# A forgetting-attention and gated feed-forward kernel with its opening rearranged: loads, fillers, gate rows and table load

## The chip, the cores and the metric

The kernel runs on one core of a Trainium2 chip. The metric is the device time of one execution in microseconds (us). TensorE (PE) multiplies matrices; VectorE (DVE), ScalarE (ACT) and GpSimd (POOL) work element by element; SyncE (SP), ACT and POOL issue DMA transfers, SP and ACT on one kind of queue and POOL on another. Each engine carries out its own instructions in the order of the program and waits on semaphores for the others.

## The reference, cut to what matters

```python
B, H, S, D = 8, 8, 576, 64                        # batches, heads, positions, head width
scores = q @ k.T / 8                              # per batch and head
cum    = cumsum(log(clip(f, 1e-4, 1)))            # along the positions
scores = where(causal, -1e9, scores + cum[:, None] - cum[None, :])
attn   = softmax(scores) @ v                      # 4608 x 512, heads side by side
g      = attn @ w_gate                            # 512 -> 1536
out    = ((g * sigmoid(g)) * (attn @ w_val)) @ w_out   # 4608 x 512, float32
```

## The kernel before

**Planning.** The kernel doesn't issue its work directly. It lists operations (`op`), each with the engines that may do it, an estimated duration, what it comes after, which buffers it takes, a key, an earliest time (`ready`) and, for a transfer, an estimated duration (`dma`). `Plan.run` then plays these through in time: an engine that is free takes the ready operation with the smallest key, and instructions are written out in that order. A table `ORDER` overrides keys of single operations. So any change of an estimate, a key or an earliest time moves the order on every engine, and the order that comes out is fixed in the program. Where PE has nothing, the plan puts in `dummy` products (L995), the fillers, from `ID_AT` on and not after `IDLE_TO`.

**Heads and pairs.** Batch 0 and batch 1 are loaded with two heads stacked on the two halves of the partitions. For batch 0, four loads `ld_quad` (L541, q and k for each of two groups) go out on POOL; each serves two pairs of heads (jj = 0, 1 for one group, 2, 3 for the other). PE transposes them piece by piece (`turn_two`, L549, 18 products of 64x64 for each pair and operand), and ACT or DVE copies the result from PSUM to the tile QK (`straighten_two`; the copy is L323 on ACT and L325 on DVE).

**Scores.** `score2` forms the scores of a pair (L708), first its first part (bank 0: keys and queries 0 to 255 as far as causal, 256 + 128 columns) and later the second part (banks 1 to 3, 1216 columns in five pieces). The decay terms are added by further products into the same bank. For the second part this is one product per piece (L716) of the key's gate rows `KG` with a tile `QG[jj]` that holds this pair's query gates; `choose` makes `QG[jj]` from the cumulative sum (L387 on ACT, L389 on DVE). For the first part there are two products (L719, L720): `KG` with a column of ones, and a one-hot column of the identity with `QS`, the scaled cumulative sum of all pairs, which one ACT instruction makes (`up`, L382). ACT takes the exponential (L724), POOL masks the diagonal blocks (L733), PE multiplies with V (`weigh`, L747), DVE divides (L754, L759), PE transposes the result (L764), and the copy to xT follows.

**Gates.** `gates` loads the gate input f of batch 0 four times into 64 partitions (`ld_f`, four transfers of 16 rows, two each on SP and ACT), clips it (DVE, L355), takes logarithms (ACT, L358), forms the cumulative sum (DVE, L362) and splits it into bfloat16 parts in `KG` (DVE, L367, L371, L375, L378), in two parts of 256 and 320 columns. f of the other six batches (`flat`, in the tile ot) takes another way: clip, logarithm, a write to memory (`regroup`, L352) and a read back in another layout (L350), then a cumulative sum and five steps (`later`) much later. SP also copies gate rows and rows of ones into QK for batch 1 (`dec_in`, L399; L477). The ones come from a fill of a part of the tile ot (L466, DVE). L517 is a tiny exponential that loads ACT's table for it ahead of use.

**Feed-forward.** For each of nine token tiles of 512: the two products with the weights (L892, four per unit), tanh on ACT (L896), two DVE steps (L900, L903), and the product with w_out (L907). Units of the first tile can run as soon as its tokens and the weights (L888) are there, and are what PE does between attention steps from then on. Later batches' q and k are narrowed in memory by POOL (`narrow`) and transposed by DMA on SP, at times set by `PACE0`, `PACE`, `PACE_A` and `LEAD`.

Of the kernel before, what the change touches and what calls it, by code (L numbers as in the profile page):

```python
# [9 lines left out]
F32 = mybir.dt.float32  # L10
# [24 lines left out]
class Plan:  # L35
# [41 lines left out]
    def run(self, idle=None):  # L77
# [31 lines left out]
        while left:  # L109
# [46 lines left out]
            for e in engines:  # L156
                while busy[e] <= t + 1e-9:
# [27 lines left out]
                    if o.dma is not None:  # L185
# [3 lines left out]
                        push(max(end + (0.2 if o.tag == "f" else 0.9), T_SW if e == "POOL" else 0.0), "queue", o)  # L189
# [27 lines left out]
PACE0 = 58.0  # L217
LEAD = 14.0
# [3 lines left out]
def kernel(ctx, tc, q, k, v, f, w_gate, w_val, w_out, out):  # L222
# [51 lines left out]
    warm = sb("warm", [1, 1], F32)  # L274
    bank = [banks.tile([P, MT], F32, name=f"ps{i}") for i in range(8)]
# [14 lines left out]
    QS = xT[:, 3, 3 * S + D : 3 * S + D + HALF]  # L290
# [90 lines left out]
    def up(e, c):  # L381
        nc.scalar.activation(QS, cum[:, c], AF.Copy, scale=8.0)  # L382

# [31 lines left out]
    def gates(parts, key):  # L415


        lds = [op(("ACT" if n % 2 else "SP", 0.45), ld_f, n, key=-40, dma=0.1, packet=100, tag="f") for n in range(4)]
        ld1 = op(("SP", 0.5), ld_f, None, key=-39, dma=LD1, packet=50, ready=LD1_AT, behind=lds[2:3], tag="f1")
# [6 lines left out]
        for i, c in enumerate(parts):  # L426
# [8 lines left out]
            u = op(("ACT", 0.15 + w / 1100), up, c, after=[s], key=kk, tag="up") if i == 0 and ONEHOT else None  # L435
            done.append([[a, o_one, u] if jj in ONEHOT and not i else
# [3 lines left out]
        outs = [op(("SP", SPi), dec_in, n, j, after=ends, key=-7 + 0.1 * j, dma=0.05, packet=50, tag="decin") for j in range(2) for n in range(4)]  # L440
# [13 lines left out]


    def blank(e, what):
# [8 lines left out]
        elif what == "ones":  # L465
            E[e].memset(ones.bitcast(F32), ONE2)  # L466
# [36 lines left out]
        else:  # L503
            if what != "rest":
                nc.vector.memset(VB[what][:, :, :, D:].bitcast(F32), ONE2)
            if what:
                nc.vector.memset(VB[0 if what == "rest" else what][LAST:, NB - 1], 0.0)
# [4 lines left out]
    o_id = op(("POOL", 0.6), lambda e: make_identity(nc, ident[:, :]), key=-18)  # L512
    o_past = op(("DVE", 0.1), blank, "past", key=-29.2)
# [5 lines left out]
    o_vb = [op(("DVE", 0.4 if i else 0.12), blank, i, key=(-29.5, VB1_KEY)[i] if i < FIRST else 40 + 2000 * i, ready=0 if i == 0 else 10 if i < FIRST else 15) for i in range(NVB)]  # L519
    o_qkz = op(("DVE", 0.3), blank, "qk", key=QKZ_KEY)  # L520
    o_pt = op(PT_ENG, blank, "pt", key=PT_KEY, ready=10)
    o_ones = op(ONES, blank, "ones", key=ONES_KEY, ready=10)
    o_edge = op(("SP", SPi), blank, "edge", after=[o_qkz], key=900, dma=0.2, ready=22)
    o_out1 = [op(("SP", SPi), blank, (w, j), after=[o_ones], key=1, dma=0.05, packet=50, ready=4) for j in range(2) for w in range(2)]
# [108 lines left out]
    def four(g, key):  # L633
# [3 lines left out]
        for j in range(2):  # L637
            jj = 2 * g + j
            q_ready[0, jj] = []
            for x in range(2):  # L640
                kk = key + STEP[j] + x
                bt = Buf("t", ("f", TURN_F))
                o2 = op(("PE", 0.41), turn_two, jj, x, bt, after=[o1[x], o_id], take=[bt], key=kk, tag=("turn", 0, jj, x))
# [52 lines left out]
    def score2(e, b, jj, i, bs):  # L696
# [14 lines left out]
        for n, (kt, q0, w, c) in enumerate(segs):  # L711
            for u in range(2):
                r, end = slice(D * u, D * (u + 1)), n == len(segs) - 1
                o, keys = ps(bs[u])[:, c : c + w], KG_ALL[r, kt * P : (kt + 1) * P]
                if i or jj not in ONEHOT:
                    nc.tensor.matmul(o, keys, QG[jj][r, q0 : q0 + w], start=False, stop=end)  # L716
# [98 lines left out]
    def attention2(b, key, parts):  # L815

        bx = {}
        for n, (bks, qb, nq) in enumerate(parts):
            ahead = len(parts) > 1 and n == 0
            got = {}  # L820
            for jj in range(4):
# [4 lines left out]
                for m, i in enumerate(bks):  # L826
                    bs = [Buf("s", ("f", F_UNTIL)) for _ in range(2)]
                    segs = [x[2] for x in BANKS[i]]
                    cost = mm(*segs) * (3 if not i and jj in ONEHOT else 2) + 0.105
# [163 lines left out]
    def dummy(i):  # L993
        z = bank[bank_of[i[0]] + i[1]]
        nc.tensor.matmul(z[:, :HALF], ident, ident.unsqueeze(1).to_broadcast([P, 2, P]), start=True, stop=True)  # L995
# [9 lines left out]
TWARM = 7.5  # L1005
ID_AT = 2.72
SPARE = 0.12
LD1_AT = 0.0
QUAD0 = (1.85, 1.25, 1.65, 1.4)
# [10 lines left out]
ONEHOT = (0, 1, 2, 3)  # L1020
CLIP1_KEY = -24.9
PT_ENG = ('DVE', 0.66)
PT_KEY = 3
ONES = ('DVE', 0.3)
# [107 lines left out]
```

## Time and profile before

| what | value |
|---|---|
| runs shown | 382.79, 383.37 and 384.94 us (median 383.37) |
| the profiled execution's own time | 382.61 us |
| its span, first to last instruction | 380.9 us |
| PE busy | 372.1 us |
| DVE, ACT, POOL busy | 218.8, 211.2, 141.2 us |
| HBM traffic over the span | 146 GB/s |

The span is 1.7 us shorter than the execution's own time, as starting and ending lie outside it. A row of a timeline has the start, the duration from the first start to the last end of a merged group, engine, line, operation, output and input, shapes, and the count; in brackets stands idle time just before it and what ended it. PE's records include the passage through the array, so rows that follow each other overlap.

### The profile page before, as it was taken

Reading aid. Unit: us, or ns where it says so; the run is one execution under the profiler, and the core shown is the slowest. Engines: PE = TensorE matmul, PEld = TensorE weight load, DVE = VectorE, ACT = ScalarE, POOL = GpSimd, SP = SyncE. Lnnn points to the kernel's source line nnn. Section 1 sums busy time; section 2 is a strip of 40 time slices with the busy share of each in tenths; the row PEclk is TensorE's granted clock in tenths of the full one; section 3 lists DMA queues with packets and bytes.
Section 4 is the critical chain, followed back from the end, with each engine's and each line's share of the span. In section 5 each row is a group of like instructions: output and inputs, shape, how many; then the busy total and the mean of one; then the engine's idle time right before and its main releaser. Section 6 shows DMA issues by size and latency. Waiting matters only on the chain.

```text
span 380.9 us, 8367 instructions
## 1 busy us (share of the span) xinstructions
PE 372.1 (98%) x3127; PEld 206.4 (54%) x3127; DVE 218.8 (57%) x458; ACT 211.2 (55%) x433; POOL 141.2 (37%) x368
## 2 busy tenths in 40 slices
PE   5999999999999999999999999999999999999997
PEld 3668555555555555545554565555654444444444
DVE  7899794467616772387327651576327815743860
ACT  5999745266566574835674577547763323323322
POOL 8896446236443463526452356513430000000000
PEclk9999999999999999999999999999999999999999
DMA  9999997997588989999799979992321011002003
GB/s 129 187 194 201 211 209 150 167 235 143 117 194 162 207 130 161 206 188 183 129 203 203 178 123 187 234 220 55 94 74 45 0 57 55 0 29 83 3 0 111
DMA packets 125319, 51.96 MB, mean 136 GB/s; under 512 B 112110, under 2 KB 119726, under 8 KB 124510
## 3 DMA queue, kind: packets, MB, share of 16 engines
q1 hardware_dynamic: 108782, 36.18, 47.8%
q0 software_dynamic: 16288, 15.14, 26.6%
q8 instruction: 24, 0.39, 0.4%
q14 instruction: 17, 0.14, 0.1%
q10 hardware_dynamic: 208, 0.11, 0.1%
HBM read 38.56 MB, written 17.07 MB: 146 GB/s over the span
## 4 chain that ended last, share of the span: by engine, by line
PE 89%; DMA 5%; ACT 2%; DVE 2%; issue 1%; POOL 1%; DVEq 0%; POOLq 0%
PE ps L892 46%; PE ps L907 25%; PE ps L690 9%; PE ps L747 7%; DMA lnf_d<-ot 4%; DMA QK<-lnf_d 1%; ACT PT L724 1%; PE ps L995 1%; PE ps L708 1%; PE ps L764 0%; DVE th L900 0%; ACT QK L323 0%; POOL xT L541 0%; PE ps L549 0%; DVE QK L362 0%
## 5 line engine op out<-in xcount | busy, mean ns | idle before, releaser
L896 ACT ACTIVATE th<-ps 128x512 f32<-128x512 f32 (+1 forms) x112 | 65.1, 582 | 83.9 <-PE ps L892 82.8
L892 PE MATMUL ps<-xT,wg 128*128 128x512 bf16 (+1 forms) x448 | 111.4, 371 | 0.2 <-DVE th L900 0.2
L892 PE MATMUL ps<-xT,wv 128*128 128x512 bf16 (+1 forms) x448 | 111.4, 371 | 0.1
L900 DVE SCALAR_TENSOR_TENSOR th<-th,ps 128x512 f32<-128x512 f32 (+1 forms) x112 | 74.6, 666 | 60.2 <-ACT th L896 59.8
L907 PE MATMUL ps<-wo,hh 128*128 128x512 bf16 (+3 forms) x468 | 105.8, 362 | 0.0
L724 ACT ACTIVATE PT<-ps 128x512 bf16<-128x512 f32 (+2 forms) x192 | 91.7, 510 | 18.6 <-PE ps L690 12.1
L903 DVE TENSOR_TENSOR hh<-th,ps 128x512 bf16<-128x512 f32 (+1 forms) x112 | 74.7, 668 | 11.8 <-PE ps L892 0.9
L733 POOL TENSOR_SCALAR_AFFINE_SELECT PT<-PT 128x128 bf16<-128x128 bf16 (+1 forms) x192 | 53.2, 282 | 55.5 <-ACT PT L724 50.4
L892 PEld LDWEIGHTS <-wv 128*128 128x128 bf16 x448 | 42.7, 97 | 41.6 <-issue 0.5
L690 PE MATMUL ps<-QK 68*128 68x256 bf16 (+4 forms) x392 | 64.8, 260 | 0.1
L892 PEld LDWEIGHTS <-wg 128*128 128x128 bf16 x448 | 42.3, 97 | 40.5 <-issue 0.5
L907 PEld LDWEIGHTS <-hh 128*128 128x128 bf16 x468 | 41.2, 97 | 34.4
L733 POOL TENSOR_SCALAR_AFFINE_SELECT PTa<-PTa 128x256 bf16<-128x256 bf16 x64 | 26.5, 418 | 85.3 <-ACT PTa L724 84.1
L754 DVE RECIPROCAL rc<-ps 128x5 f32<-128x5 f32 (+2 forms) x68 | 12.9, 190 | 68.3 <-PE ps L747 68.1
L911 ACT ACTIVATE ot<-ps 128x512 f32<-128x512 f32 (+3 forms) x39 | 22.0, 565 | 45.2 <-PE ps L907 43.7
L747 PE MATMUL ps<-VB,PT 128*128 128x65 bf16 x768 | 45.1, 193 | 0.0
L747 PEld LDWEIGHTS <-PT 128*128 128x128 bf16 x768 | 36.8, 97 | 14.4 <-POOL PT L733 1.3
L690 PEld LDWEIGHTS <-QK 68*128 68x128 bf16 x392 | 31.4, 97 | 17.2 <-issue 0.4
L724 ACT ACTIVATE PTa<-ps 128x384 bf16<-128x384 f32 x64 | 30.8, 488 | 14.3 <-PE ps L690 13.2
L759 DVE TENSOR_TENSOR xn<-ps,rc 128x320 bf16<-128x320 f32 (+2 forms) x72 | 32.2, 453 | 2.1
L325 POOL CAST VB<-natv 128x512 bf16<-128x512 f32 (+1 forms) x32 | 19.7, 631 | 0.0
L747 PEld LDWEIGHTS <-PTa 128*128 128x128 bf16 x192 | 13.1, 97 | 11.3 <-issue 1.1
(71 smaller groups left out, 153.2 us busy)
## 6 DMA issues: line engine op xcount, KB each, us to landing
out_dram<-ot SPq DMA_DIRECT2D x35, 256.0 KB
natv<-in_v_dram SPq DMA_DIRECT2D x25, 256.0 KB
qk_d<-in_q_dram POOLq DMA_DIRECT2D x24, 144.0 KB, 3.8
qk_d<-in_k_dram POOLq DMA_DIRECT2D x24, 144.0 KB, 4.4
wg<-in_moe_w_gate_dram POOLq DMA_DIRECT2D x3, 512.0 KB, 12.1
wv<-in_moe_w_val_dram POOLq DMA_DIRECT2D x3, 512.0 KB, 13.5
wo<-in_moe_w_out_dram POOLq DMA_DIRECT2D x4, 384.0 KB, 16.7
xT<-in_q_dram POOLq DMA_DIRECT2D x4, 288.0 KB, 8.8
```

What stands on the lines that cost most here:

```text
L325: E[e].tensor_copy(dst, src)
L690: nc.tensor.matmul(s[:, c : c + w], QK[:KR, hqk[p].i, 1, j * S + kt * P : j * S + (kt + 1) * P], QK[:KR, hqk[p].i, 0, j * S + q0 : j * S + ...
L724: nc.scalar.activation(place(h, i)[:, OFFS[i] : OFFS[i] + c], ps(bs)[:, :c], AF.Exp, scale=0.125)
L733: nc.gpsimd.affine_select(out=d, in_=d, pattern=pat, compare_op=ALU.is_ge, fill=0.0, base=0, channel_multiplier=-1,)
L747: nc.tensor.matmul(o[:, lo : lo + D + 1], pt[:, c : c + P], VB[hvb[b].i][:, kt, hb, : D + 1], start=first and n == 0, stop=last and n == l ...
L759: nc.vector.tensor_mul(XN[bx.i][:, qb : qb + nq, j], o, r)
L892: nc.tensor.matmul(ps(bf)[:, :n], w[:, ko, fc * P : (fc + 1) * P], xT[:, ko, t0 : t0 + n], start=(ko == 0), stop=(ko == KD - 1))
L896: nc.scalar.activation(TH[bt.i][:, :n], ps(bf)[:, :n], AF.Tanh, scale=0.5)
L900: nc.vector.scalar_tensor_tensor(out=t, in0=t, scalar=1.0, in1=ps(bf)[:, :n], op0=ALU.add, op1=ALU.mult)
L903: nc.vector.tensor_mul(HH[bh.i][:, lo : lo + n], TH[bt.i][:, :n], ps(bf)[:, :n])
L907: nc.tensor.matmul(ps(bf)[:m, c], HH[hs[fc].i][:, lo : lo + m], wo[:, fc, c], start=(fc == 0), stop=(fc == KF - 1))
L911: nc.scalar.activation(OT[bo.i][:m, c], ps(bf)[:m, c], AF.Copy, scale=0.5)
```

## The change

- Loads of f for batch 0: two transfers of 32 rows (a source that repeats the 16 rows), one on SP and one on ACT, in place of four of 16.
- The fillers read a new tile `idle`, filled by DVE at the start, in place of the identity; `ID_AT` goes from 2.72 to 0.8.
- `ONEHOT1 = (0, 1)`: pairs 0 and 1 take the two-product form in the second part too. A second `QS` is made by a second `up`, and `choose` is left out for these two pairs in that part.
- Fills can be done by ACT (`fill32`): the ones rows go to ACT in the resulting order; the padding of the second V buffer stays on DVE and comes earlier.
- The round trip of the other batches' logarithms may start earlier (`ready` 6 and 16 in place of 21 and 27).
- Estimates of the plan: PE's `turn_two`, the warm-up time, the time from issue to queue of the f loads, issue times of SP, load times; `PACE0` 57 for 58 and `LEAD` 16 for 14; a new `ORDER` table.

The order that results differs on every engine. At the start it is, by line of the new kernel (which are 8 to 10 higher): POOL issues k and q of the first group, makes the identity, issues q and k of the second, four chunks of V, then batch 1's first loads; before it was q, a chunk of V, k, identity, q, k and the rest of V. ACT does four logarithms, the ones fill, the logarithm for the other batches, the table load, then a copy, `up`, five copies, the second `up`, two exponentials, a copy and exponentials; before, the table load came after two copies. SP issues one ones row, the write L353, three ones rows, five gate rows, the read L351, three gate rows, then V loads. PE has 18 fillers ahead of the first transposes (11 before), 35 in all (22), and the first product of the feed-forward comes after more of the attention.

```diff
-                        if o.tag[0] != "turn":
-                            dur *= self.clock(t)
+                        dur *= self.clock(t)
...
-                        push(max(end + (0.2 if o.tag == "f" else 0.9), T_SW if e == "POOL" else 0.0), "queue", o)
+                        push(max(end + (0.7 if o.tag == "f" else 0.9), T_SW if e == "POOL" else 0.0), "queue", o)
...
-PACE0 = 58.0
-LEAD = 14.0
+PACE0 = 57.0
+LEAD = 16.0
...
+    idle = sb("idle", [P, P], BF16)
...
-    QS = xT[:, 3, 3 * S + D : 3 * S + D + HALF]
+    QS = [xT[:, 3, 3 * S + D : 3 * S + D + HALF], xT[:, 0, 2 * S : 3 * S - HALF]]
...
-        E[e].dma_start(out=lf[2 * H * c : 2 * H * (c + 1)], in_=f.rearrange("b h s -> (b h) s")[: 2 * H])
+        src = bass.AP(f.tensor, f.offset, [[0, 2], [S, 2 * H], [1, S]])
+        E[e].dma_start(out=lf[4 * H * c : 4 * H * (c + 1)], in_=src)
...
-        nc.scalar.activation(QS, cum[:, c], AF.Copy, scale=8.0)
+        nc.scalar.activation(QS[c.start > 0], cum[:, c], AF.Copy, scale=8.0)
...
-            u = op(("ACT", 0.15 + w / 1100), up, c, after=[s], key=kk, tag="up") if i == 0 and ONEHOT else None
-            done.append([[a, o_one, u] if jj in ONEHOT and not i else
+            u = op(("ACT", 0.15 + w / 1100), up, c, after=[s], key=kk, tag="up") if (ONEHOT, ONEHOT1)[i] else None
+            done.append([[a, o_one, u] if jj in (ONEHOT, ONEHOT1)[i] else
...
-        a = op(("SP", 0.5), regroup, False, after=[l1], key=1, dma=0.5, packet=40, ready=21, tag="regroup")
+        a = op(("SP", 0.5), regroup, False, after=[l1], key=-50, dma=0.5, packet=40, ready=6, tag="regroup")
         regrouped.append(a)
-        l1 = [l1, op(("SP", 0.5), regroup, True, after=[a], key=1, dma=0.4, packet=100, ready=27, tag="regroup")]
+        l1 = [l1, op(("SP", 0.5), regroup, True, after=[a], key=2, dma=0.4, packet=100, ready=16, tag="regroup")]
...
+    def fill32(e, t, x):
+        if e == "ACT":
+            z = ct[:, 0:1]
+            src = bass.AP(z.tensor, z.offset, [[z.ap[0][0], t.shape[0]]] + [[0, n] for n in t.shape[1:]])
+            nc.scalar.activation(t, src, AF.Copy, scale=0.0, bias=x)
+        else:
+            E[e].memset(t, x)
...
-            E[e].memset(ones.bitcast(F32), ONE2)
+            fill32(e, ones.bitcast(F32), ONE2)
...
+    op(("DVE", 0.12), lambda e: nc.vector.memset(idle.bitcast(F32), ONE2), key=-1e5)
...
-                if i or jj not in ONEHOT:
+                if jj not in (ONEHOT1 if i else ONEHOT):
                     nc.tensor.matmul(o, keys, QG[jj][r, q0 : q0 + w], start=False, stop=end)
                 else:
                     mine = D * u + 6 * H + FB * u + jj
                     nc.tensor.matmul(o, keys, one[r, jj : jj + 1].to_broadcast([D, w]), start=False, stop=False)
-                    nc.tensor.matmul(o, ident[r, mine : mine + 1].to_broadcast([D, P]), QS[r, q0 : q0 + w], start=False, stop=end)
+                    nc.tensor.matmul(o, ident[r, mine : mine + 1].to_broadcast([D, P]), QS[i > 0][r, q0 - (HALF if i else 0) : q0 - (HALF if i else 0) + w], start=False, stop=end)
...
-        nc.tensor.matmul(z[:, :HALF], ident, ident.unsqueeze(1).to_broadcast([P, 2, P]), start=True, stop=True)
+        nc.tensor.matmul(z[:, :HALF], idle, idle.unsqueeze(1).to_broadcast([P, 2, P]), start=True, stop=True)
...
-TWARM = 7.5
-ID_AT = 2.72
+TWARM = 7.0
+ID_AT = 0.8
...
+ONEHOT1 = (0, 1)
```

More of the change, by code (lines that the diff above doesn't have):

```diff
@@ L415, in gates @@
     def gates(parts, key):
-        lds = [op(("ACT" if n % 2 else "SP", 0.45), ld_f, n, key=-40, dma=0.1, packet=100, tag="f") for n in range(4)]
-        ld1 = op(("SP", 0.5), ld_f, None, key=-39, dma=LD1, packet=50, ready=LD1_AT, behind=lds[2:3], tag="f1")
+        lds = [op(("ACT" if n else "SP", 0.6), ld_f, n, key=-40, dma=0.2, packet=100, tag="f") for n in range(2)]
+        ld1 = op(("SP", 0.5), ld_f, None, key=-39, dma=LD1, packet=50, ready=LD1_AT, behind=lds[:1], tag="f1")
         done, s, lns = [], None, []
@@ L518 @@
     o_rest = op(("DVE", 0.3), blank, "rest", key=QKZ_KEY + 0.1)
-    o_vb = [op(("DVE", 0.4 if i else 0.12), blank, i, key=(-29.5, VB1_KEY)[i] if i < FIRST else 40 + 2000 * i, ready=0 if i == 0 else 10 if i < FIRST else 15) for i in range(NVB)]
+    o_vb = [op({"DVE": 0.4, "ACT": 0.6} if i == 1 else ("DVE", 0.4 if i else 0.12), blank, i, after=[o_ct] if i == 1 else [], key=(-29.5, VB1_KEY)[i] if i < FIRST else 40 + 2000 * i, ready=0 if i == 0 else 4.5 if i < FIRST else 15) for i in range(NVB)]
     o_qkz = op(("DVE", 0.3), blank, "qk", key=QKZ_KEY)
     o_pt = op(PT_ENG, blank, "pt", key=PT_KEY, ready=10)
-    o_ones = op(ONES, blank, "ones", key=ONES_KEY, ready=10)
+    o_ones = op(ONES, blank, "ones", after=[o_ct], key=ONES_KEY, ready=4.5)
     o_edge = op(("SP", SPi), blank, "edge", after=[o_qkz], key=900, dma=0.2, ready=22)
-    o_out1 = [op(("SP", SPi), blank, (w, j), after=[o_ones], key=1, dma=0.05, packet=50, ready=4) for j in range(2) for w in range(2)]
+    o_out1 = [op(("SP", 0.64), blank, (w, j), after=[o_ones], key=1, dma=0.05, packet=50, ready=4) for j in range(2) for w in range(2)]
     o_out2 = [op(("SP", SPi), blank, x, after=[o_ones], key=1, dma=0.36, packet=50, ready=ONES_AT) for x in ("ones_q", "ones_k")]
@@ L1023 @@
 PT_KEY = 3
-ONES = ('DVE', 0.3)
+ONES = {'DVE': 0.3, 'ACT': 0.32}
 ONES_KEY = 3
```

12 lines of the change are left out of this document (6 added, 6 removed), and 106 rows, old and new, of the table ORDER.

## The prediction

> **What bounds the kernel now.** I read the page's head and slices first, then busy time by stretch, then the timelines of the first 16 us, the chain of waits and the waits by line.
>
> ```profile
> span 380.9 us, 8367 instructions
> ...
> PE   5999999999999999999999999999999999999997
> ```
>
> ```profile
> 0.00:12.00 12.00, 6.82 (x136) 4.73 (x138) 9.91 (x43) 7.85 (x15) 10.30 (x18) 1.00 1.04 139
> 12.00:24.00 12.00, 11.56 (x233) 7.87 (x230) 9.92 (x47) 11.58 (x28) 11.40 (x28) 1.00 1.47 198
> 24.00:36.00 12.00, 11.89 (x199) 9.56 (x199) 11.25 (x30) 11.15 (x25) 9.92 (x25) 1.00 1.47 190
> ```
>
> Columns of the second view: length, busy time and count of PE, weight loads, DVE, ACT and POOL, then clock, DMA share and GB/s. From 24 us on PE has no free time worth the name, so the end is PE's whole work plus what PE loses before that. "Busy" hides small gaps, because each product's record includes its passage through the array. The pitch is the better measure:
>
> ```profile
> 284.85 20.72 PE ps L892 x96
> ...
> 14.63 0.39 PE L708 MATMUL ps<-QK 64*128 64x192 bf16 x4
> 14.86 0.38 PE L716 MATMUL ps<-xT 64*128 64x192 bf16 x4
> ...
> 24.07 1.04 PE L892 MATMUL ps<-xT,wg 128*128 128x256 bf16 x8
> ```
>
> 96 products of 512 columns in 20.72 us are 0.216 us each, a column per 1/2400 us and 2.5 ns more. The four products at 14.63 (192 and 320 columns, once for each half of the array) take 0.23 us to the next row: 1024 columns would be 0.43, so products on the two halves run side by side. Adding up widths with that pitch, in the program's order, from the first score product at 11.79 (below) to the first L892 at 24.07 gives 8.8 us of streaming in 12.3 us: PE loses 3.4 us there, in gaps that no row names. In this stretch ACT is busy 11.58 of 12 us (exponentials and copies): ACT sets the pace of the first attention, and before 12 us it is the loads and ACT's list that hold PE.
>
> ```profile
> 3.96 1.86 ACT L358 ACTIVATE xT<-xT 64x256 f32<-64x256 f32 x4 [0.74 <-DVE xT L355]
> 5.73 0.40 ACT L382 ACTIVATE xT<-xT 128x256 bf16<-128x256 f32 x1
> 7.68 1.19 ACT L323 ACTIVATE QK<-ps 128x576 bf16<-128x576 bf16 x2 [1.55 <-PE ps L549]
> 8.76 0.38 ACT L358 ACTIVATE ot<-ot 128x216 f32<-128x216 f32 x1
> 9.16 1.28 ACT L517 ACT_TABLE_LOAD   x1
> ...
> 10.57 0.64 ACT L387 ACTIVATE xT<-xT,ct 128x320 bf16<-128x320 f32 x1
> 11.11 1.69 ACT L323 ACTIVATE QK<-ps 128x576 bf16<-128x576 bf16 x3
> 12.70 0.46 ACT L724 ACTIVATE PTa<-ps 128x384 bf16<-128x384 f32 x1
> ...
> 13.61 1.96 ACT L724 ACTIVATE PTa<-ps 128x384 bf16<-128x384 f32 x5
> ```
>
> The reader is to see one hole on ACT, the 1.55 us before 7.68, and that table load, selection and three copies stand between it and the first exponential at 12.70.
>
> **The change part by part.** Six parts; the sum follows.
>
> *Fillers from 1.5 us.* The fillers read a small tile that DVE sets instead of the identity, so PE starts after about four fills of DVE rather than at 4.50; 22 fillers become 35.
>
> ```profile
> 4.50 2.53 PE L995 MATMUL ps<-ident 128*128 128x256 bf16 x11 [4.50 <-POOL ident masks.py:199]
> 6.95 0.99 PE L549 MATMUL ps<-ident,xT 64*64 64x64 bf16 x36
> 7.87 1.16 PE L995 MATMUL ps<-ident 128*128 128x256 bf16 x5
> ...
> 9.78 0.83 PE L995 MATMUL ps<-ident 128*128 128x256 bf16 x6
> ...
> 9.19 0.55 PEld L549 LDWEIGHTS <-xT 64*64 64x64 bf16 x36 [0.55 <-DMA xT<-in_k_dram]
> 10.62 0.55 PEld L549 LDWEIGHTS <-xT 64*64 64x64 bf16 x36 [0.29 <-DMA xT<-in_q_dram]
> 11.79 0.34 PE L708 MATMUL ps<-QK 64*128 64x256 bf16 x4 [0.51 <-ACT QK L323]
> ```
>
> A filler takes 0.21 us until after 8 us and 0.11 from 9.78: PE is at half speed for some 4 us after its start, whatever the profile's clock column says. With the start at 1.5 it should be fast by 6, and the first 36 transposes take 0.6 instead of 0.9 us. That 0.3 us is hidden here (ACT is at its logarithms and table load then; without that cover it is 0.3), so I count 0. The Trainium skill, "TensorE: Matmul & The Clock Gate", Part 1, says that some 3.4 us of sustained work raise the clock and an idle window of that length lowers it. The trace shows the rise, about 4 us late; no run here shows the fall, which would be against this change (a rival below).
>
> *Order of the loads.* POOL now issues both loads of the first two pairs, then the identity, both of the other two, and only then V. Between 9.19 and 10.62 stands one load of 288 KB: 1.43 us. The first, V's 128 KB (0.64 at that rate) and k landed by 9.19, so the first landed by about 9.19 - 2.07 = 7.1, and PE's 6.95 agrees. In the new order they land at 6.9, 8.3, 9.8 and 11.2.
>
> *ACT's list.* Now the four logarithms, the fill of the ones rows (from DVE), the logarithm for the other batches and the table load all come ahead of the first copy.
>
> ```profile
> 3.58 0.35 DVE L355 TENSOR_SCALAR xT<-xT 64x256 f32<-64x256 f32 x1 [0.41 <-DMA xT<-in_f_dram]
> ...
> 5.59 0.38 DVE L367 TENSOR_SCALAR xT<-xT 128x256 bf16<-128x256 f32 x1
> ...
> 7.36 0.48 DVE L378 SCALAR_TENSOR_TENSOR xT<-xT,ct 128x256 bf16<-128x256 f32 x1
> ...
> 8.32 0.87 DVE L362 TENSOR_TENSOR_SCAN xT<-xT 128x320 f32<-128x320 f32 x1
> ...
> 9.46 1.40 DVE L389 TENSOR_SCALAR xT<-xT,ct 128x320 bf16<-128x320 f32 x3
> 10.78 0.74 DVE L325 COPY QK<-ps 128x576 bf16<-128x576 bf16 x1
> ...
> 12.01 0.55 DVE L371 SCALAR_TENSOR_TENSOR xT<-xT,ct 128x320 f32<-128x320 bf16 x1
> ...
> 13.54 0.57 DVE L378 SCALAR_TENSOR_TENSOR xT<-xT,ct 128x320 bf16<-128x320 f32 x1
> 14.81 0.30 DVE L466 MEMSET ot<- 64x288 f32 x1
> ```
>
> DVE has two fills more ahead of the first clip, so logarithms start at about 4.3 (3.96 before) and end at 6.05 (1.77 as before). The ACT fill has no row: between the 0.30 of DVE's and the 0.47 of a 320-wide logarithm (1.86 for four); 0.35, nearer DVE's, gives 6.4. Logarithm to 6.8 (8.76 to 9.16), table and warm-up 1.41 (9.16 to 10.57) to 8.2. The first copy then waits for the second load and its transposes: 8.3 + 0.4 = 8.7. A copy costs 0.53 (three from 11.11 to 12.70), the scaled cumulative sum 0.40. Copy, sum, copy: 10.2. The third load's copies are ready at 9.8 + 0.7 = 10.5, so 0.3 is lost; four more copies end at 12.6 (the last load, 11.2 + 0.5, is in time), the second part's sum at 13.0, and the first exponential starts there: 0.3 later than now. But at 13.0 ACT has done six copies where it now has done five, and takes a seventh that DVE has now. With two exponentials of 0.37 and that copy it stands at 14.3; the same list now (13.61 + 0.37 + 0.53) would be 14.5, and DVE has 0.74 less. ACT's lead is 0.2 to 0.5; I take 0.35.
>
> DVE's chain of the first gate rows starts after all four logarithms and a copy: 7.95 instead of 5.59, plus 2.25 (5.59 to 7.84) gives 10.2, in time for score products that start at about 10.2. The second part: scan 0.87, scale, one selection 0.44 instead of three (1.40 / 3), 0.66 of fills moved ahead, then 2.1 (12.01 to 14.11): 14.5, now 14.1. The score that needs them stands behind all four pairs' first scores, at about 15. That cover is 0.5 us; without it the delay is 0.4.
>
> *One more product each.* Pairs 0 and 1 get their second part's gates from two products instead of one: five widths, 192 + 320 + 64 + 320 + 320 = 1216 columns, for two pairs and on both halves: 20 products, 2 x 1216 / 2400 + 0.02 = 1.04 us of PE. They fall between 15 and 21 us, where PE loses part of 3.4 us behind ACT. Bounds: 0 and 1.04. I take 0.2, near the lower, since ACT is 11.58 of 12 there. In exchange one selection of ACT (0.54, 10.57 to 11.11) and one of DVE go, and ACT gets the 0.40 counted above.
>
> *The round trip for the later batches.* Written and read back ahead of time: the write leaves SP behind the first ones row, at some 7 us, not at 24.
>
> ```profile
> 24.04 13.71 DMA lnf_d<-ot
> 37.77 4.79 DMA QK<-lnf_d
> 42.58 1.37 DVE QK L362
> ...
> DVE QK L362 <- DMA QK<-lnf_d: 1.4, 1, 1.4
> ...
> 44.58 1.02 PE L892 MATMUL ps<-xT,wg 128*128 128x512 bf16 x4 [0.17 <-DVE th L900]
> ```
>
> DVE's 1.4 us stall goes; behind it stood L900, and PE waited 0.17 us for that, with as much again in gaps to 48. Gain 0.2 to 0.6; I take 0.45.
>
> *Later start of the feed-forward.* In the new order the first L892 comes after 13.5 us of the present PE work, not 10.8. The present kernel has that much done at some 27 us. Filler products are what closes PE's gaps; without them for 3 us PE loses at the rate of 12 to 24 (0.28 per us) rather than of 24 to 36 (0.1): 0 to 0.5, taken as 0.2.
>
> Sum: -0.35 + 0.2 - 0.45 + 0.2 = -0.4 us on a profiled execution of 382.6 (span 380.9 and 1.7 around it): 382.2. The median of the runs shown is 383.4, 0.8 above it, so between the two I forecast a median of 382.9. A 0.5% step is 1.9 us, about what a measurement here can tell from no change: the forecast lies within.
>
> **The rivals.**
> (A) *Clearly faster, 381.0.* ACT and DVE share the copies, and both are over 11 of 12 us busy from 24 to 36. The 1.55 hole and DVE's relief (0.74 + 0.30 + 0.44) make 3.0 us; halved, 1.5 sooner, the stall 0.45, the extra products fully covered: about -2.0. For it: the busy shares. Against: the new walk has holes too (0.5 before the first copy, 0.3 after).
> (B) *Slower: the early write holds SP's ring, 386.* The write took 13.71 us among other loads. SP's eight gate-row copies for batch 1 stand around it, the fifth behind its landing and three behind the read (4.79). At 7 + 13.7 the last row lands at 20.7 + 0.7 + 4.8 + 2.3 = 28.5. The first score of batch 1 (L690) stands now at about 30. From there on each us is a us of an in-order PE; a write of 18 us costs 3. For it: the same ring, and the loads are as dense at 7 us. Against: nothing big is queued ahead of it on SP's ring there. The Trainium skill, "DMA: Bandwidth & Descriptors", Queues, rings and completion order, has the engines take turns between queues by packets, which would slow the write only by a share; no row here separates queues.
> (C) *The clock falls back, 383.7.* From 5.4 to 10 PE has only 9 fillers and the transposes. At half speed from 8 to 13, the first four scores (2.1 us of streaming) take 4.2; ACT hides most, 0.8 remains.
> (D) *The reordering moves nothing, 383.4*: the first copy waits for its load, the last lands as now.
>
> **How the numbers follow.** Forecast 0.52, A 0.22, B 0.14 (with any other late arrival in the new order), C 0.06, D 0.06. Faster by over 0.5%: A, 0.22. Slower: B and a rest, 0.16. Same: 0.62. The likeliest case alone spans 381.7 to 384.2 (its terms' bounds: -1.1 to +1.3); the range takes in A's body and the edge of B: 380.6 to 385.4.
>
> **What would show it.** Right: first exponential at 12.7 to 13.2; no ACT hole before the first copy over 0.8; PE's first filler by 1.7; the read-back landed before 30 and no DVE wait on it; first L902 near 26. Wrong: PE waits on a gate row's load at 28 to 34 (B); fillers of 0.21 us after 7 us (C); a PE stall after 60, which nothing above foresees.

## The result, and the profile after

The change makes the kernel slower: 387.79 us (387.67 to 388.99, six runs) against 382.8 us (381.77 to 384.94, six runs), a ratio of 1.0129 with a 95% interval of 1.0101 to 1.0158. Ratios, here and below, leave out the few executions that took over 1.5% longer than the fastest of the same kernel. The forecast was 382.9, with a range up to 385.4. The profiled execution took 387.67 us; its span is 5.1 us longer than before.

The page of the kernel after, its head and the queue that brings the program in (packets, MB, share of 16 engines):

```profile
span 386.0 us, 8368 instructions
...
q8 instruction: 25, 0.41, 0.4%
```

Busy time by stretch, kernel after, columns as in the forecast's second view:

```profile
0.00:12.00 12.00, 7.84 (x120) 5.31 (x122) 6.85 (x40) 6.47 (x13) 9.04 (x17) 1.00 1.04 142
12.00:24.00 12.00, 12.00 (x215) 7.84 (x207) 8.59 (x40) 9.85 (x24) 8.45 (x17) 1.00 1.43 206
```

DVE did 6.85 us of work before 12 us where it had done 9.91, ACT 6.47 where it had done 7.85. From 12 to 24 PE is "busy" all 12.00 us, yet carries out 215 products instead of 233. Both are explained by the timeline of the opening, kernel after:

```profile
0.81 1.24 ACTq L346 DMA_DIRECT2D xT<-in_f_dram  x1
0.81 0.82 SPq L346 DMA_DIRECT2D xT<-in_f_dram  x1
...
1.41 4.02 PE L1005 MATMUL ps<-idle 128*128 128x256 bf16 x18 [1.41 <-DVE idle L522]
...
6.61 0.52 DVE L356 TENSOR_SCALAR xT<-xT 64x320 f32<-64x320 f32 x2 [2.80 <-DMA xT<-in_f_dram]
...
8.19 0.99 PE L559 MATMUL ps<-ident,xT 64*64 64x64 bf16 x36 [2.75 <-DMA xT<-in_k_dram]
...
9.16 1.28 ACT L527 ACT_TABLE_LOAD   x1
...
10.56 0.62 ACT L323 ACTIVATE QK<-ps 128x576 bf16<-128x576 bf16 x1
...
15.74 0.50 PE L718 MATMUL ps<-QK 64*128 64x256 bf16 x4
...
16.92 0.49 ACT L734 ACTIVATE PTa<-ps 128x384 bf16<-128x384 f32 x1 [0.90 <-PE ps L730]
```

Two things went wrong. First, f is late. The clip starts at 6.61, not 3.58, after DVE has waited 2.80 us for f. ACT's table load is at 9.16, its first copy at 10.56 instead of 8.7. The same goes for POOL's first load, of k: it takes 6.8 us from issue to landing (4.7 with f as before, in e1 below), and PE's first transposes wait 2.75 us for it. Second, PE is at half speed until about 17 us: the transposes take 0.99 us per 36 (0.66 when fast, below), four scores 0.50 us at 15.74 where the first four before took 0.34 at 11.79. ACT, which set the pace before, now waits for PE: 0.90 us ahead of the first exponential, at 16.92 instead of 12.70.

By the working of the forecast (streaming of the products issued so far, in program order, taken from the time) PE has lost 17.2 us by 36 us, against 14.5 before: +2.7. From 42 to 48 us it loses 0.4 instead of 0.9, as the wait for the read-back is gone. The extra products add 1.04 us of streaming. That is +3.2 us, and the last copies show the same, before and then after (timeline of the end):

```profile
371.03 7.63 SPq L914 DMA_DIRECT2D out_dram<-ot  x6
...
377.51 0.92 ACT L911 ACTIVATE ot<-ps 128x128 f32<-128x128 f32 x3 [0.24 <-PE ps L907]
```

```profile
374.24 8.83 SPq L924 DMA_DIRECT2D out_dram<-ot  x6
...
380.73 0.92 ACT L921 ACTIVATE ot<-ps 128x128 f32<-128x128 f32 x3 [0.24 <-PE ps L917]
```

The last three copies start 3.22 us later; from there to the end of the span, the tail, it is 3.4 us before and 5.3 after. 3.2 and 1.9 make the 5.1. Three losses are thus to be explained: f's delay, the slow clock, and a longer tail.

### The profile page after: what moved, and what is told of

Read it like the earlier page. It is cut to its first block, busy times and chain, and to the rows that moved or that the text cites. A ratio compares the mean times of both kernels' runs of the same rounds, so it can differ in the third digit from the quotient of the medians.

```text
span 386.0 us, 8368 instructions
## 1 busy us (share of the span) xinstructions
PE 374.7 (97%) x3113; PEld 209.5 (54%) x3160; DVE 216.5 (56%) x454; ACT 212.7 (55%) x437; POOL 138.7 (36%) x368
## 4 chain that ended last, share of the span: by engine, by line
PE 96%; DMA 2%; issue 1%; ACT 0%; POOLq 0%
PE ps L902 48%; PE ps L917 24%; PE ps L700 10%; PE ps L757 8%; DMA xT<-in_k_dram 2%; PE ps L718 1%; PE ps L1005 1%; PE ps L559 1%; PE ps L774 1%; PE ps L575 1%; PE ps L729 1%; PE ps L730 1%; PE ps L726 0%; ACT PT L734 0%; ACT PTa L734 0%
## 5 line engine op out<-in xcount | busy, mean ns | idle before, releaser
L902 PE MATMUL ps<-xT,wg 128*128 128x512 bf16 (+1 forms) x435 | 110.3, 371 | 0.6
L902 PE MATMUL ps<-xT,wv 128*128 128x512 bf16 (+1 forms) x434 | 109.9, 371 | 0.8
L917 PE MATMUL ps<-wo,hh 128*128 128x512 bf16 (+3 forms) x448 | 102.5, 362 | 0.9
L734 ACT ACTIVATE PT<-ps 128x320 bf16<-128x320 f32 (+2 forms) x192 | 91.3, 512 | 15.9 <-PE ps L700 10.4
L913 DVE TENSOR_TENSOR hh<-th,ps 128x512 bf16<-128x512 f32 (+1 forms) x112 | 74.7, 668 | 13.2 <-PE ps L902 3.0
L743 POOL TENSOR_SCALAR_AFFINE_SELECT PT<-PT 128x128 bf16<-128x128 bf16 (+1 forms) x192 | 51.6, 275 | 54.8 <-ACT PT L734 49.1
L902 PEld LDWEIGHTS <-wg 128*128 128x128 bf16 x448 | 42.6, 97 | 41.1
L902 PEld LDWEIGHTS <-wv 128*128 128x128 bf16 x448 | 42.5, 97 | 40.7
L700 PE MATMUL ps<-QK 68*128 68x256 bf16 (+2 forms) x392 | 63.5, 261 | 0.1
L757 PE MATMUL ps<-VB,PT 128*128 128x65 bf16 x768 | 43.0, 193 | 0.1
L757 PEld LDWEIGHTS <-PT 128*128 128x128 bf16 x768 | 35.3, 97 | 12.9 <-issue 0.9
L325 POOL CAST VB<-natv 128x512 bf16<-128x512 f32 (+1 forms) x32 | 18.8, 612 | 0.8 <-DMA natv<-in_v_dram 0.8
## 6 DMA issues: line engine op xcount, KB each, us to landing
wo<-in_moe_w_out_dram POOLq DMA_DIRECT2D x4, 384.0 KB, 13.3
```

The source lines that it names most:

```text
L325: E[e].tensor_copy(dst, src)
L700: nc.tensor.matmul(s[:, c : c + w], QK[:KR, hqk[p].i, 1, j * S + kt * P : j * S + (kt + 1) * P], QK[:KR, hqk[p].i, 0, j * S + q0 : j * S + ...
L734: nc.scalar.activation(place(h, i)[:, OFFS[i] : OFFS[i] + c], ps(bs)[:, :c], AF.Exp, scale=0.125)
L743: nc.gpsimd.affine_select(out=d, in_=d, pattern=pat, compare_op=ALU.is_ge, fill=0.0, base=0, channel_multiplier=-1,)
L757: nc.tensor.matmul(o[:, lo : lo + D + 1], pt[:, c : c + P], VB[hvb[b].i][:, kt, hb, : D + 1], start=first and n == 0, stop=last and n == l ...
L902: nc.tensor.matmul(ps(bf)[:, :n], w[:, ko, fc * P : (fc + 1) * P], xT[:, ko, t0 : t0 + n], start=(ko == 0), stop=(ko == KD - 1))
```

## Experiments

All ratios are to the kernel before on the same chip. Profiles are single executions, up to 1.5 us from their kernel's median, so verdicts rest on ratios and profiles tell where.

**f by four plain transfers in the kernel after (e1).**

```diff
-        src = bass.AP(f.tensor, f.offset, [[0, 2], [S, 2 * H], [1, S]])
-        E[e].dma_start(out=lf[4 * H * c : 4 * H * (c + 1)], in_=src)
+        for n in (2 * c, 2 * c + 1):
+            E[e].dma_start(out=lf[2 * H * n : 2 * H * (n + 1)], in_=f.rearrange("b h s -> (b h) s")[: 2 * H])
```

> The changed kernel with f of batch 0 in four transfers of 16 rows again, all else in the new order. Theory T (transfer): the two repeating transfers of 32 rows land at 6.6 us instead of 3.6, and delay the first load too; here the clip's wait ends at about 3.6 to 3.9, the first transposes start at about 7, the first exponential at 13 to 14, and the time falls by 2 to 3 us from 387.8 to 385 or 386. Theory C (clock): PE stays at half speed to 16.8 as before whatever f does, so the time falls by less than 0.7. Theory O (the new order and its 1.04 us more of products): f is covered by the wait for the first load, 387.8 stays within 0.5.

Measured 385.61 us (384.63 to 386.54), ratio 1.0066 [1.0041, 1.0092]: half of the loss is gone. Timeline of e1, and then its PE by stretch (length, PE busy and count, granted clock, DMA share, GB/s):

```profile
3.90 0.60 DVE L356 TENSOR_SCALAR xT<-xT 64x320 f32<-64x320 f32 x2
...
6.02 0.66 PE L559 MATMUL ps<-ident,xT 64*64 64x64 bf16 x36 [0.69 <-DMA xT<-in_k_dram]
...
9.47 0.99 PE L559 MATMUL ps<-ident,xT 64*64 64x64 bf16 x36 [0.82 <-DMA xT<-in_q_dram]
...
13.68 0.50 PE L718 MATMUL ps<-QK 64*128 64x256 bf16 x4
...
14.86 0.87 ACT L734 ACTIVATE PTa<-ps 128x384 bf16<-128x384 f32 x2 [0.90 <-PE ps L730]
```

```profile
4.00:8.00 4.00, 2.87 (x81) 1.00 1.20 198
8.00:10.00 2.00, 1.18 (x38) 0.63 1.19 174
10.00:12.00 2.00, 2.00 (x40) 0.50 2.08 186
12.00:14.00 2.00, 2.00 (x50) 0.50 2.12 174
14.00:16.00 2.00, 2.00 (x25) 0.67 1.28 204
```

f is there at 3.90. PE is fast at 6.02, and then the clock falls back: here the granted clock says it itself, 0.50 from 10 to 14. (In the kernel after it stands at 1.00 throughout although the products take double. The trace's record of the clock begins with a rise, at 17.08 us there and at 8.81 in the kernel before; ahead of its first entry the column shows 1.00.) In e1 the record has a rise at 5.10, a fall at 8.51 and a rise at 15.34.

**More early fillers in the kernel after (e2), and both edits together (e3).** The first 18 fillers are issued twice (`turns_out` is empty until the first transposes).

```diff
-        nc.tensor.matmul(z[:, :HALF], idle, idle.unsqueeze(1).to_broadcast([P, 2, P]), start=True, stop=True)
+        for _ in range(2 if len(turns_out) == 0 else 1):
+            nc.tensor.matmul(z[:, :HALF], idle, idle.unsqueeze(1).to_broadcast([P, 2, P]), start=True, stop=True)
```

> The changed kernel with each filler ahead of the first transposes issued twice (36 in place of 18), so that PE has work from 1.4 us to about 7 to 8. Theory C: PE is at full speed before the first transposes and stays so, the first scores' products run 0.34 in place of 0.50, and the time falls by 0.7 to 1.5 us to 386.3 to 387.1. Theory T: PE still waits for the first load at 8.2 and ACT for f; only the cold products' share comes back, 0 to 0.5 us. Theory O: nothing.

> Both edits together. If T and C are two separate losses they add: 387.8 - 2.5 - 0.9 = 384.4. If the early f by itself closes PE's gap and warms it, the same as e1. Theory O: 387.8.

e2: 386.2 us (384.91 to 388.03 in nine runs, a tenth took 390.77), ratio 1.0094 [1.0063, 1.0124]. e3: 383.87 us (383.12 to 385.24), 1.0027 [1.0001, 1.0052]. Timelines of e2 and of e3:

```profile
8.39 0.66 PE L560 MATMUL ps<-ident,xT 64*64 64x64 bf16 x36 [0.95 <-DMA xT<-in_k_dram]
...
17.38 0.21 PE L720 MATMUL ps<-QK 64*128 64x128 bf16 x1 [1.68 <-issue]
```

```profile
3.92 0.58 DVE L356 TENSOR_SCALAR xT<-xT 64x320 f32<-64x320 f32 x2
...
9.54 0.66 PE L560 MATMUL ps<-ident,xT 64*64 64x64 bf16 x36 [0.68 <-DMA xT<-in_q_dram]
...
10.57 0.34 PE L720 MATMUL ps<-QK 64*128 64x256 bf16 x4
...
12.86 0.90 ACT L736 ACTIVATE PTa<-ps 128x384 bf16<-128x384 f32 x2
```

With f early and PE fast, the first exponential is at 12.86, inside the 12.7 to 13.2 of the forecast, and PE's loss by 36 us is 14.5, that of the kernel before. Of the 1.29% about 1.0 belongs to these two. By the ratios they give 2.4 us for f alone, 1.3 for the fillers alone and 3.9 for both. The 1.3 is not the price of the clock alone: in e2's profile PE starts fast at 8.39, but stands still for 1.68 us ahead of 17.38, for nothing that the profile shows, and its clock is at half speed from 19.06 to 22.47. e3's profile, its slowest run, has a wait of PE of 1.64 us for one late transfer, ahead of 182.62.

**The repeating transfers alone, in the kernel before (e4).**

```diff
-        E[e].dma_start(out=lf[2 * H * c : 2 * H * (c + 1)], in_=f.rearrange("b h s -> (b h) s")[: 2 * H])
+        if c < 2:
+            src = bass.AP(f.tensor, f.offset, [[0, 2], [S, 2 * H], [1, S]])
+            E[e].dma_start(out=lf[4 * H * c : 4 * H * (c + 1)], in_=src)
```

> The kernel before with f of batch 0 in the two repeating transfers of 32 rows, all else in its own order. Theory T: f lands 2 to 3 us later (clip at about 6), and the kernel before loses 1.5 to 3 us: 384.5 to 386 against 382.8. Theory O: it loses less than 0.5, since in this order ACT has a hole of 1.55 us that takes it up.

387.98 us (387.25 to 388.31), 1.0113 [1.0064, 1.0162], more than expected. Timeline of e4:

```profile
0.81 1.23 ACTq L347 DMA_DIRECT2D xT<-in_f_dram  x1
...
7.15 0.34 DVE L357 TENSOR_SCALAR xT<-xT 64x256 f32<-64x256 f32 x1 [3.99 <-DMA xT<-in_f_dram]
...
8.58 0.99 PE L551 MATMUL ps<-ident,xT 64*64 64x64 bf16 x36 [1.60 <-DMA xT<-in_q_dram]
...
15.11 0.50 PE L710 MATMUL ps<-QK 64*128 64x256 bf16 x4 [0.97 <-ACT QK L323]
...
16.29 0.49 ACT L726 ACTIVATE PTa<-ps 128x384 bf16<-128x384 f32 x1 [0.17 <-PE ps L722]
```

One edit of the change, put into the kernel before, costs as much as the whole change. It costs both things at once: f at 7.15, and scores of 0.50 us at 15.11 (the clock's first entry is a rise at 21.80); the first load is late too, its transposes at 8.58 instead of 6.95. It is not the same loss, though: e4's last copies start 5.05 us later than before and its tail is 3.7 us, and in the changed kernel this edit is about half (e1).

**Thirty-two different rows instead of a repeated sixteen (e8).** The edit is in the kernel after; half of the 64 rows then belong to other batches, so the output is another one.

```diff
-        src = bass.AP(f.tensor, f.offset, [[0, 2], [S, 2 * H], [1, S]])
+        src = bass.AP(f.tensor, f.offset, [[S, 4 * H], [1, S]])
```

> The changed kernel with its two transfers of f reading 32 different rows in place of 16 rows twice (so the gates of half the heads are those of other heads, and the output is not the reference's). If the repeated source makes them late, f lands near 4 and the time is like that with four transfers, 385.6; if it is the size of the transfers (32 rows of 2.3 KB, whole rows as packets, and a longer issue), f lands at 6.5 again and the time is 387.8.

One run, 386.25 us, span 384.5. Timeline of e8:

```profile
0.81 0.42 ACTq L346 DMA_DIRECT2D xT<-in_f_dram  x1
...
3.74 0.76 DVE L356 TENSOR_SCALAR xT<-xT 64x320 f32<-64x320 f32 x2
```

The same bytes in as many transfers are there at 3.74, like e1. So it is not the size of 32 rows that makes f late but the form of the source, three levels with a zero step in front (no run has three levels without the zero). The first 10 us of ACT's queue, which carry its half of f alone, say what differs; before, after and e8 in this order (packets, MB, share of 16 engines):

```profile
q10 hardware_dynamic: 64, 0.07, 2.2%
```

```profile
q10 hardware_dynamic: 34, 0.07, 1.9%
```

```profile
q10 hardware_dynamic: 48, 0.07, 1.9%
```

Each time 32 rows of 2304 bytes are moved. The rest is 2 x 16 packets for two transfers, 2 for the repeating one, 16 for the plain one of 32 rows: a packet for each engine that takes part, on this reading, and the repeating transfer runs on two. The Trainium skill, "DMA: Bandwidth & Descriptors", Rules for kernel authors, says just this: a leading step of zero with c copies confines a transfer to at most c engines. The counts agree; no row here names the engines. Also by rows, the issue takes 0.82 and 1.24 us instead of 0.41 and 0.42, and by 3 us all 64 packets had moved in the kernel before, 5 of 34 in the kernel after. From then on POOL's loads move beside them (the first of theirs falls into that same third microsecond). The records of single packets say more. The 64 rows of f, on both queues, move from 1.83 to 2.88 us in the kernel before and from 1.84 to 2.68 in e8, with up to 16 and 18 of them under way at once. In the kernel after they move from 2.82 to 6.02, never more than 4 at once, ACT's 32 first and SP's behind them. That bears out few engines, and says why DVE waits until 6.61 for the half on SP.

**The extra products alone, in the kernel before (e5).** Pairs 0 and 1 take two products per piece in the second part; the selection becomes one scaled sum.

```diff
-        nc.scalar.activation(QS, cum[:, c], AF.Copy, scale=8.0)
+        nc.scalar.activation(QS[c.start > 0], cum[:, c], AF.Copy, scale=8.0)
...
-                if i or jj not in ONEHOT:
+                if i and jj not in (0, 1):
```

> The kernel before with the second part's gates of pairs 0 and 1 by two products each, the place of one selection given to the scaled sum and the other selection left out; all else in its own order. Covered by ACT (the prediction's step): PE's loss before 24 us falls by about as much as the 1.04 us that the products cost, and the time rises by 0 to 0.4 us. Not covered: 1.04 us more, 383.5 against 382.5.

382.9 against 382.68 us, ratio 0.9986 [0.9959, 1.0014]. In this order the 20 products are covered, to within 0.5 us.

**The earlier fillers alone, in the kernel before (e10).** The tile `idle`, and 14 more fillers from 1.4 us on.

```diff
-        nc.tensor.matmul(z[:, :HALF], ident, ident.unsqueeze(1).to_broadcast([P, 2, P]), start=True, stop=True)
+        calls.append(i)
+        for _ in range(15 if len(calls) == 1 else 1):
+            nc.tensor.matmul(z[:, :HALF], idle, idle.unsqueeze(1).to_broadcast([P, 2, P]), start=True, stop=True)
```

> The kernel before with a small tile for the fillers as in the changed kernel, and 14 fillers more at the start (from 1.4 us); f, loads and order as they were, 6284 rows. Clock theory: PE is fast before its first transposes at 6.95 (x36 in 0.66 instead of 0.99), the first copy comes 0.3 sooner, and the time falls by 0 to 0.4 us, to 382.1 to 382.6, unless the wait for k's load at 9.2 takes it back.

383.28 us (381.79 to 385.89), 1.0007 [0.9972, 1.0042]: no difference. In the profile PE is fast from its first transposes on (0.66 us at 6.80), the first exponential at 12.41 instead of 12.70. On the whole that part was costed rightly at about nothing. Its runs are not alike, though. Six of the twelve have a granted clock of 1.0 and a median of 382.4 us; four have 0.987 to 0.991, some 7 to 10 us at half speed by an estimate from these shares, and took 383.85 to 385.54.

**A longer program in the kernel before (e6).** Its first 11 fillers become 44 products of one column: PE's program is 6322 rows long (two for each product), as after, instead of 6256.

```diff
+        if not turns_out:
+            for _ in range(4):
+                nc.tensor.matmul(z[:1, :1], ident[:, :1], ident[:, :1], start=True, stop=True)
+            return
```

> The kernel before with each of its first eleven fillers replaced by four products of one column, so that PE's program has as many rows as the changed kernel's (66 more); the work is the same. If the longer tail of the changed kernel (5.3 us from the start of the last three copies to the end, 3.4 before) comes from a block of PE's program that is fetched while the last stores are issued, a 25th fetch shows up on that queue in the last 6 us and the tail grows by 1 to 2 us, to 383.5 to 384.5. If the tail comes from something else in the changed kernel, it stays at 3.4 and the time within 0.5 of 382.5 (the first transposes stay at half speed in both cases).

386.16 us (385.0 to 387.01), 1.0069 [1.0041, 1.0097], much more than a tail. Timeline of e6:

```profile
4.49 1.24 PE L999 MATMUL ps<-ident 128*1 128x1 bf16 x44 [4.49 <-POOL ident masks.py:199]
...
5.94 0.99 PE L550 MATMUL ps<-ident,xT 64*64 64x64 bf16 x36 [0.22 <-DMA xT<-in_q_dram]
...
15.78 0.50 PE L710 MATMUL ps<-QK 64*128 64x256 bf16 x4
...
373.49 8.42 SPq L916 DMA_DIRECT2D out_dram<-ot  x6
...
379.98 0.92 ACT L913 ACTIVATE ot<-ps 128x128 f32<-128x128 f32 x3 [0.24 <-PE ps L909]
```

The edit did two things. It took the full fillers away, and with f on time and the transposes even earlier PE stays at half speed to 21.13 us, the first rise on record (8.81 before): the last copies come 2.5 us later, which is what a slow clock alone costs here. And from the last copies to the end it is 4.4 us (span 384.4), 1.0 more than before, with a 25th packet of program.

**Three fillers fewer after (e9).** PE's program gets 6316 rows (`calls` lists the fillers so far).

```diff
+        calls.append(i)
+        for _ in range(0 if len(calls) <= 3 else 1):
```

> The changed kernel with three of its eighteen first fillers left out, so that PE's program has 6316 rows in place of 6322; runs of 6318 rows and fewer had 24 blocks fetched on the instruction queue, those of 6322 and more 25. If the fetched block makes the tail, there are 24, the tail from the last copies falls from 5.3 to 3.4 or 3.7 and the time by 1.5 to 1.9, to 386 to 386.3, with the first 380 us as they were. If the tail has another cause, 387.8 stays.

386.94 us (385.92 to 387.97), 1.0109 [1.0057, 1.0161]: by its interval not different from the kernel after. In its profile the span is 384.0 with 24 packets of program; the last copies start at 379.96, so the tail is 4.0 us against 5.3, though not the 3.4 of before.

**Twenty-four early fillers (e11), the one-product gates again in e3 (e7), and in e11 (e12).** e11 is e1 with the first six fillers doubled and the last eight left out.

```diff
-        nc.tensor.matmul(z[:, :HALF], idle, idle.unsqueeze(1).to_broadcast([P, 2, P]), start=True, stop=True)
+        calls.append(i)
+        for _ in range(2 if len(calls) <= 6 else 0 if len(calls) > 27 else 1):
+            nc.tensor.matmul(z[:, :HALF], idle, idle.unsqueeze(1).to_broadcast([P, 2, P]), start=True, stop=True)
```

e7 and e12 add:

```diff
-        nc.scalar.activation(QS[c.start > 0], cum[:, c], AF.Copy, scale=8.0)
+        if c.start:
+            choose("ACT", 0, c)
+        else:
+            nc.scalar.activation(QS[0], cum[:, c], AF.Copy, scale=8.0)
...
+        if c.start:
+            choose("DVE", 1, c)
...
-                if jj not in (ONEHOT1 if i else ONEHOT):
+                if i:
```

> The changed kernel with f in four transfers, the first fillers doubled, and the second part's gates of pairs 0 and 1 by one product each again (one selection on ACT in place of the second scaled sum, one more on DVE). If the products cost their 1.04 us in this order, 382.8 against 383.9 for the same without this edit; if ACT covers them, 383.9 or more, since ACT and DVE get 0.2 and 0.44 us. A wait of PE on late gate rows of a later pair (1.6 us near 190 us in the run with both edits) may stand in its way or go.

> The changed kernel with f in four transfers, 24 first fillers in place of 18 and without the last eight fillers: 6318 rows, 24 blocks. If the transfers, the clock and the tail are the three losses, this has none of them: PE fast through the first scores (0.34), tail 3.4 to 3.7, and 387.8 - 2.2 - 1.7 = 383.9 less up to 1.0 of tail: 382.5 to 383.9. If the clock falls back without the last fillers, some 385.

> The changed kernel with f in four plain transfers, 24 early fillers and none of the last eight, and one-product gates again for pairs 0 and 1 of the second part: 40 rows of PE's program fewer than the same without the last edit (6278, so between the 6256 of before and the 6322 of after). Theory that the tail grows with PE's program reaching its 25th block: 24 blocks, 3.4 to 3.7 us from the start of the last three copies to the end, last copies at 377.0 to 377.8, a span of 380.5 to 381.4, a ratio of 0.998 to 1.002. Rival (the tail depends on something else of the change, such as the order of loads and stores on SP's queue): a tail of 4.2 us or more and a span over 381.6 with 24 blocks. If the kernel is no faster than before although f is early, PE warm and PE's program short, nothing of the change is left that pays.

e7: 384.4 us (383.0 to 385.38), 1.0029 [1.0008, 1.0051], no better than e3: in its profile the 36 fillers hold the first transposes up until 7.94 us (6.75 in e3, with as many). e11: 384.11 us (383.44 to 386.62), 1.0035 [1.001, 1.0059]. e12: 382.97 us (381.64 to 384.97), 0.9999 [0.9971, 1.0027]. Timelines of e11 and of e12:

```profile
1.41 4.20 PE L1008 MATMUL ps<-idle 128*128 128x256 bf16 x24 [1.41 <-DVE idle L522]
...
9.77 0.66 PE L559 MATMUL ps<-ident,xT 64*64 64x64 bf16 x36 [0.82 <-DMA xT<-in_q_dram]
...
378.00 0.92 ACT L922 ACTIVATE ot<-ps 128x128 f32<-128x128 f32 x3 [0.24 <-PE ps L918]
```

```profile
12.35 0.86 ACT L740 ACTIVATE PTa<-ps 128x384 bf16<-128x384 f32 x2
...
376.28 0.92 ACT L927 ACTIVATE ot<-ps 128x128 f32<-128x128 f32 x3 [0.24 <-PE ps L923]
```

e11 differs from e1 by six fillers in the opening (the eight it leaves out come behind the first transposes of all four pairs), and has the same wait of 0.82 us ahead of its third transposes, yet stays fast. e12 brings the change to the time of the kernel before, and no further. Its tail is 3.6 us (span 379.9) with 24 packets; e11's is 4.8 (span 382.8) with 25, where 24 and at most 3.7 were expected. By the ratios 1.4 us lie between e11 and e12. They may be the 1.04 us of products, the tail, or chance: the intervals overlap, and e7 gained nothing on e3. So e5's answer holds for the old order alone.

*Which executions are slow is in part chance.* Where the early fillers raise the clock (in the profile of the kernel after they don't), the rise comes 2.7 us (e3) to 5.4 us (e10) after the first of them, and 18 fillers last some 4.0 us. Of the ten profiles with fillers from 1.4 us, the four with 15 or 18 (after, e1, e8, e9) are at half speed at 13 us; the six with 24 or more (e2, e3, e7, e10, e11, e12) are not. Of e1's ten runs five show a clock of 0.991, as its profile does; of e3's ten none is below 0.999, of e11's twelve none below 0.996.

*The tail, what is shown and what not.* Kernels with PE programs of up to 6296 rows (before, e4, e5, e10, e12) have 24 packets and tails of 3.4 to 3.7 us. Those of 6318 to 6322 rows with 25 packets (after, e1, e6, e8, e11) have 4.4 to 5.4, and e2 with 6358 has 4.2. But e7 with 6318 rows (24 packets) has 3.7, e9 4.0, and e3, with 6358 rows and 25 packets, only 3.6. In e6 a longer program goes with 1.0 us more at the end, in e3 a still longer one with 0.2. These are single profiles: that the length of the program is the cause is not shown, and what decides was not settled.

## Why the prediction was wrong

*The step that failed* stands in the walk along ACT's list: "DVE has two fills more ahead of the first clip, so logarithms start at about 4.3". It took f's landing over from the row at 3.58 although the transfers that bring f had another form. Two transfers in place of four stood in the diff, which also raises the plan's own estimate for f, from issue to queue, from 0.2 to 0.7 us; they had no term in the sum. They moved the clip to 6.61 and the logarithms to 6.96, 2.7 us later than forecast; with f in four transfers they start at 4.34 (e1), as forecast. Everything behind them on ACT moved too: first copy 10.56 for 8.7. And they moved the first load, forecast to land at 6.9: its transposes waited until 8.19. e4 has this part alone at 1.0113, e8 shows that the form of the source makes it. The page of the Trainium skill that the forecast named under rival B has the rule for it; the forecast took another rule from that page.

*Rival C was right in kind and wrong in size and chance.* It named the place (few fillers from 5.4 to 10) and the sign (half-speed products after 7 us), and gave 0.8 us at 0.06. e6 has a slow PE to 21 us with f on time, and its last copies come 2.5 us later. The 0.8 assumed that ACT hides most of it; the rows say that ACT waits for PE (0.90 us at 16.92). And the clock was slow for longer, to about 17 us rather than 13. The late transfers and the slow clock hang together: with the first load late, PE stood idle for 2.75 us behind its fillers. The forecast said no run showed the fall; e1 does, at 8.51, 3.41 us after the rise, with no idle stretch of PE over 0.69 us between the two. So the idle window of some 3.4 us that the forecast cited was not needed for it. The Trainium skill, "TensorE: Matmul & The Clock Gate", Part 4: PE-mode transpose, says that transposes do not count as busy work in the same way. That would fit e1: from 6.02 to 9.47 PE had transposes and six fillers, and fell back. But e11 had the same from 6.13 to 9.77, behind six more fillers, and did not, and no run here tells transposes from other products.

*The tail* had no term at all, and measured +1.9 us in the one profile.

*Right, by their own rows.* The loads came no later than forecast once f was in time: in e11 the first three transposes start at 6.13, 7.74 and 9.77 for landings at 6.9, 8.3 and 9.8. (The forecast read the first landing before off the row at 6.95, which shows no wait for a load; in e6 the same transposes start at 5.94, behind such a wait.) ACT's list behind them was right: first exponential 12.97 in e11 for 13.0, and two of them and a copy done at 14.24 for 14.3. The extra products: forecast 0.2 out of 0 to 1.04, and e5 leaves 0 to 0.5 in the old order. The early fillers: 0 forecast, e10 shows none on the whole. The round trip: forecast -0.45; no wait precedes DVE's L363 at 44.98, and PE's loss from 42 to 48 us fell by 0.5. Rival B did not happen: the write leaves at 9.65, the read at 19.56, and no PE wait on gate rows follows. The first L902 was forecast near 26; it came at 31.38 after, at 28.71 in e11, 27.07 in e12. So it moved with the opening; what its later start cost by itself no run separates.

*No rival A either.* With both faults mended and the extra products out, the first exponential is at 12.35 (e12, 12.70 before), and PE's loss by 36 us is 14.1 against 14.5; the time is still that of before. What little is won at the start is below what the medians here can tell.

## What to carry to other kernels

When a diff makes fewer transfers of the same bytes, price the form of each transfer, above all its outermost dimension, before taking its landing time over from the old rows. Where the first microseconds of PE are fillers, count them as a term: what is moved away from the opening may leave PE slow for the next ten microseconds, and where PE is the bound most of such a loss is still there at the end (3.1 us lost by 36 us in e6, 2.5 at its last copies). Put the parts of a change into the old kernel one by one, and take them out of the new one: here one line cost the old kernel as much as the whole change, and leaving it out of the new one gave back half.

## What was not expected of the hardware

- A source that repeats 16 rows by a zero step: issue 0.82 to 1.24 us instead of 0.41, 34 packets instead of 48, at most 4 rows under way at once instead of 18, and f 3 us later on land (6.61 against 3.74, e8). A load on another queue lands 2.1 us later beside it (6.8 us after its issue against 4.7, e1).
- 44 products of one column in 1.24 us do not make PE fast: transposes 0.99 us from 5.94 to 11.32 and scores 0.50 at 15.78 (e6), while 18 to 36 fillers of 256 columns did so by 6 to 7 us (e1, e3, e10, e11); with 2.75 us of idle time behind them 18 did not (after, 8.19).
- The clock column of a profile can read 1.00 while products take double, ahead of the first change on record (17.08 us after, 21.80 in e4, 21.13 in e6).
- PE can fall back to half speed 3.41 us after it has become fast, without an idle stretch of over 0.69 us (e1).
- The tail behind the last copies is 3.4 to 5.4 us in these kernels; a longer program of PE often goes with a longer tail (e6), not always (e3), and the cause is open.
